# First sequence of a Fourier and feed-forward kernel: E as a spare row of Q, even products and table loads in another order

## The chip, the cores and the metric

The kernel runs on one core of one Trainium2 chip. The core has five engines that each work through their own queue in order: TensorE (PE, matrix products), VectorE (DVE), ScalarE (ACT), GpSimd (POOL) and SyncE (SP, which here only issues transfers). The metric is the time on the device in microseconds (us), the median over several executions. A profile is one execution recorded by the hardware profiler.

## The reference

What is computed, with eight sequences of 3008 rows and 256 columns:

```python
X = np.fft.fft(x, axis=1)
X = np.fft.fft(X, axis=2)
x = X.real.astype(np.float32).reshape(24064, 256)
h = x @ w_in            # 256 x 2048
r = np.maximum(h, 0.0)
g = r * r
out = (g @ w_out).astype(np.float32)   # 2048 x 256
```

## The kernel before, in words

**The mathematics.** Of the two Fourier transforms only the real part is wanted. The one along the columns is put into the weights: `G1` and `G2` (128 x 2048) are `w_in` multiplied by a cosine table `cosd` and a sine table `sind`. The one along the rows is done for each sequence as three arrays with 1505 columns, half of the frequencies: `Pt` (128 rows, cosine), `Qt` (127 rows, sine) and `Et`. E is the transform of one column of x alone (column 128, `H`), and it is needed on all 128 rows, because it enters the hidden layer as E times a number per row, `gE`. The hidden layer of a block of 251 columns and of 128 of the 2048 units is then `G1 . Pt` plus and minus `G2 . Qt` plus `gE * Et`; plus and minus give two output rows each.

**The transform of a sequence.** The rows of x are loaded four at a time (`load_x`, L145), as seven tiles: four tiles of even rows in three classes (`class_tiles`, L49) and three tiles, 4 to 6, of odd rows. `fold` (L352) adds and subtracts them on DVE into tiles `w`; a fold has a half for P (`for_p`: `f_s`, `f_sc`, `f_w`) and one for Q (`for_q`: `f_d`, `f_dc`, `f_w`). `dft_ops` (L447) makes from `w` and the tables `cosT` and `sinT` the groups of the transform. One group is for one of P, E, Q (`which` 0, 2, 1) and for even or odd frequencies (`kp`). It has five steps: `even_n` (L470), products of the even rows into one PSUM tile of the pool `psd`, tag "d", which has two buffers, and a copy `da` on ACT; `join_4` and `join_2` (L486 to L494), sums and differences on DVE; `odd_n` (L496), products of the odd rows into a PSUM tile of tag "h"; and `join_1` (L532), which writes the result. For E in the first sequence the same column of `w` is broadcast to 128 (L466), so that the product has E on all its rows. For the other seven sequences E is computed once for all, written to a DRAM tile `e_dram` (L548) and loaded with a broadcast (`load_e`, L551).

**Weights.** The weights come as 64-bit numbers and are rounded to 32 bits by `convert` (L230): two operations on DVE (L241, L246), three on ACT (L243, L244, L248), three on DVE (L251, L253, L254). `begin_win(j)` (L260) starts that for one of eight pieces of `w_in`, and issues its load unless it is loaded already, as pieces 0 to 2 are; `rounded(j)` ends it; then come products with `cosd` and `sind` (L269), copies `G` (L270), and two products with one column of the unit matrix for `gE` (L278). Pieces of `w_out` are loaded and converted by `load_wout` (L286).

**The order of the first sequence.** From L730 on the order is written out by hand; each engine keeps it. `awake(n)` (L193) puts n products of the unit matrix, whose result nobody uses, into PE's queue. `groups_at` calls steps by number: 0 to 9 are P, 10 to 19 E, 20 to 29 Q, five for each kp. The core of it:

```python
    load_table(cosT, cos_s, (0,))        # behind load_x(0, 4)
    ...
    groups_at(0, 5)                      # P, even products
    awake(12)
    ...
    groups_at(10, 15, 4)                 # E, even products; P, last join
    ...
    groups_at(9, 13, 18, 11, 12, 16, 17, 14)
```

**Steps.** A step works on one block of 251 columns and two times 128 hidden units (`j`, eight of them). `front` (L555) makes two pairs of products `ph` (L565, L566) and on DVE `he` (L568) and two `g` (L570, L571); the first `he` needs the first 251 columns of `Pt`, `Qt` and `Et`, and `gE`. `combine` (L578) has relu and square on ACT (L580, L581). `back` (L596) multiplies by `w_out`, two steps later; from the second block on with seven products instead of eight, whose sums of `g` are made on POOL (L588 to L591). In the first eight steps `weights` (L802) also converts the remaining pieces: in step 0 it ends piece 2 of `w_in` and begins piece 3, in step 1 it begins the first piece of `w_out` and piece 4, and so on. In all later steps the folds and groups of the next sequence are spread between the steps.

**Transfers.** Nearly all are issued by SP, one after the other; `cosd`, `sind` and its last column by ACT. A transfer signals on one of eight semaphores in turn, and the issue waits until the one before it on the same semaphore has landed. For the first sequence SP issues x tiles 0, 1, the first weights, x tiles 2 to 4, then the tables of cosine between x tiles 5 and 6, the rest of cosine, sine, and weights as their buffers come free.

Of the kernel before, what the change touches and what calls it, by code (L numbers as in the profile page):

```python
# [12 lines left out]
PSUM = bass.MemoryType.PSUM  # L13
P = 128
R = 32

# [63 lines left out]
def kernel(  # L82
# [100 lines left out]
                                     in_=src[mine[0]:mine[0] + step * (m - 1) + 1:step, :, i, 0:nk])  # L183

    make_identity(nc, ident)
    ramp = const.tile([P, 2], F32, name="ramp")
    nc.vector.memset(ramp[:, 0:1], 1151.0)
    nc.vector.memset(ramp[:, 1:2], 255.0 * 2.0 ** 23)
# [71 lines left out]
    def begin_win(j):  # L260

        w = ep.tile([P, 2, CH], F32, name="win", tag="sB" if j % 2 else "sA")
        finish = convert(parts(w, 1), win.pop(j, None) or load(pair_in(j)))

        def products():
            for tab, G, nm in ((cosd, G1, "mC"), (sind, G2, "mD")):
                pg = psm.tile([P, CH], F32, name="pg", tag=nm)
                for i in range(2):
                    nc.tensor.matmul(pg, tab[:, i], w[:, i], start=i == 0, stop=i == 1)  # L269
                nc.scalar.copy(G.rearrange("p (h j f) -> j p h f", h=2, j=NJ)[j],  # L270
                               pg.rearrange("p (h f) -> p h f", h=2))

        def for_e():

            ps = psd.tile([P, CH], F32, name="pe", tag="d")
            for h in range(2):
                fc = j + NJ * h
                nc.tensor.matmul(ps[:, h:h + 1], G2[:, fc * P:(fc + 1) * P], ident[:, P - 1:], start=True, stop=True)  # L278

            return lambda: nc.vector.tensor_scalar_mul(gE[:, j::NJ], ps[:, 0:2], 0.5)  # L280

        win[j] = finish, products, for_e
# [48 lines left out]
    NE = B - 1  # L331
    xe = const.tile([P, 4, NT, NE], F32, name="xe")
    we = const.tile([P, 2, NT, NE], F32, name="we")
    e_dram = dp.tile([NE, NKT], F32, name="e_dram")
    nc.gpsimd.memset(xe, 0.0)

    def load_column(t):
# [14 lines left out]
    def fold(b, t):  # L352
# [42 lines left out]
        def f_w(part=slice(0, D)):  # L395
            v, w = st["sc"], w_of(t)
            for kp in range(2):
                tt(out=w[r, kp, part], in0=v[r, 0, part], in1=v[r, 1, part], op=ALU.subtract if kp else ALU.add)

        if b == 0:  # L400
            return [f_s, f_d, f_sc, f_dc, lambda: f_w(PART[0]), lambda: f_w(PART[1])]
        ops = [(0.9, f_s), (0.9, f_d), (0.7, f_sc), (0.6, f_dc), (1.1, f_w)]
        if not odd or t == ODD0:
            return ops, None
# [42 lines left out]
    def dft_ops(b):  # L447
# [2 lines left out]

        def start():
            PQE[b] = [pq.tile([n, NKT], F32, name=nm, tag=nm)
                      for nm, n in (("Pt", P), ("Qt", P - 1), ("Et", P))]

        def group(kp, which):
            n = NE if b is None else P - 1 if which == 1 else P
            tab = sinT if which == 1 else cosT
            n2, _, n1, n0 = NC[kp]
            st = {}

            def product(ps, c):
                ts = [t for t in range(NT) if TILES[t][0] == c]
                for t in ts:
                    rows = TILES[t][3]
                    w = we[0:rows, kp, t] if b is None else folded[b, t][0:rows, kp, PART[which % 2]]
                    w = w[:, H:H + 1].to_broadcast([rows, n]) if which == 2 and b is not None else w[:, 0:n]  # L466
                    nc.tensor.matmul(ps, w, tab[0:rows, kp, PLACE[t]:PLACE[t] + NC[kp][c]],  # L467
                                     start=t == ts[0], stop=t == ts[-1])

            def even_n():  # L470
                st["ps"] = psd.tile([P, 512], F32, name="pd", tag="d")[0:n]
                a = st["a"] = hp.tile([P, 2 * P], F32, name="da", tag="da", bufs=2)[0:n]
                for c, at, nk in ((0, 0, n2), (1, n2, n2), (2, 2 * n2, n1)):
                    product(st["ps"][:, at:at + nk], c)
                nc.scalar.copy(a[:, 0:n2], st["ps"][:, 0:n2])

            def both(lo, hi, a, ps):

                nk, nh = a.shape[-1], hi.shape[-1]
                tt(out=lo, in0=a, in1=ps, op=ALU.add)  # L480
                if which == 1:
                    tt(out=hi[:, ::-1], in0=ps[:, 0:nh], in1=a[:, 0:nh], op=ALU.subtract)
                else:
                    tt(out=hi[:, ::-1], in0=a[:, 0:nh], in1=ps[:, 0:nh], op=ALU.subtract)
# [8 lines left out]
                st["c"] = hp.tile([P, NC[0][3]], F32, name="dc2", tag="dc2", bufs=2)[0:n, 0:n0]  # L493
                both(st["c"][:, 0:n1], st["c"][:, n1:n0], a, ps[:, 2 * n2:2 * n2 + n1])  # L494

            def odd_n():  # L496

                pool, tag = (psh, "h") if b == 0 else (psd, "d")
                ps = pool.tile([P, 512], F32, name="pd", tag=tag)[0:n]
                st["odd"] = ps[:, 0:n0]  # L500
                if not b:
                    return product(ps[:, 0:n0], 3)
                nq = (n0 + 2) // 2 if kp else (n0 + 1) // 2
                for part in range(2):
                    if kp:
                        tab, o = (cosT, sinT)[part], 0
                        to = ps[:, part * nq:part * nq + nq]
                        other = part != which
                    else:
                        tab, o = (cosT, sinT)[which], part  # L510
                        to = ps[:, part:n0:2]
                        other = part != which
                    for i, pair in enumerate(((ODD0, ODD0 + 1), (ODD0 + 2, NT))):
                        nc.tensor.matmul(to, folded[b, pair[other]][:, kp, PART[which]][:, 0:n],  # L514
                                         columns(tab, ODD0 + i, o), start=i == 0, stop=i == 1)
                if kp:
                    st["cos"] = hp.tile([P, nq], F32, name="oc", tag="oc", bufs=1)[0:n]
                    nc.scalar.copy(st["cos"], ps[:, 0:nq])
                    st["sin"] = ps[:, nq:2 * nq]
# [9 lines left out]
                else:  # L529
                    tt(out=o[:, 1::2], in0=a[:, 1:nq], in1=ps[:, 1:nq], op=ALU.subtract)  # L530

            def join_1():  # L532
                dst = PQE[1][2][0:n] if b is None else PQE[b][which]
                nh = S // 8
                both(dst[:, kp:kp + 2 * n0 - 1:2], dst[:, M - kp - 2 * (nh - 1):M - kp + 1:2], st["c"],
                     st["odd"])

            ops = [(0.1, even_n), (0.4, join_4), (0.5, join_2), (0.1, odd_n), (0.8, join_1)]
            if b and kp:
                ops.insert(4, (0.5, join_odd))  # L540
            return ops

        ops = [] if b is None else [(0.0, start)]
        for which in (2,) if b is None else (0, 1) if b else (0, 2, 1):
            for kp in range(2):
                ops += group(kp, which)
        if b is None:
            ops.append((0.0, lambda: nc.sync.dma_start(out=e_dram[:, :], in_=PQE[1][2][0:NE])))  # L548
        return ops

    def load_e(b):  # L551
        nc.sync.dma_start(out=PQE[b][2], in_=e_dram[b - 1:b].to_broadcast([P, NKT]))


    def front(b, k0, n, j, between):  # L555
# [4 lines left out]
        for h in range(2):  # L560
            fc = j + NJ * h
            fs = slice(fc * P, (fc + 1) * P)
            ps = psh.tile([P, 2, CH], F32, name="ph", tag="h")
            hP, hQ = ps[:, 0, 0:n], ps[:, 1, 0:n]
            nc.tensor.matmul(hP, G1[:, fs], pt[:, ks], start=True, stop=True)  # L565
            nc.tensor.matmul(hQ, G2[0:P - 1, fs], qt[:, ks], start=True, stop=True)  # L566
            t = hp.tile([P, CK], F32, name="he", tag="he")[:, 0:n]
            nc.vector.scalar_tensor_tensor(out=t, in0=et[:, ks], scalar=gE[:, fc:fc + 1], in1=hP,  # L568
                                           op0=ALU.mult, op1=ALU.add)
            tt(out=g[:, h, 0, 0:n], in0=t, in1=hQ, op=ALU.add)  # L570
            tt(out=g[:, h, 1, 0:n][:, ::-1], in0=t, in1=hQ, op=ALU.subtract)  # L571
            between()
# [162 lines left out]
    for_p(1)  # L735
    begin_win(0)
    load_x(0, 2)
    for dst, src in ((cosd, cos_d), (sind[:, :, 0:P - 1], sin_d), (sind[:, :, P - 1:], alt_d)):
        nc.scalar.dma_start(out=dst, in_=src.rearrange("(c p) m -> p c m", p=P))
    load_x(0, 3)  # L740
    load_x(0, 4)
    load_table(cosT, cos_s, (0,))
    load_x(0, 5)
    load_table(cosT, cos_s, (1,))
    load_x(0, 6)
    load_table(cosT, cos_s, range(2, NT))
    load_table(sinT, sin_s, range(ODD0, NT))
    win[1] = load(pair_in(1))
    load_table(sinT, sin_s, range(ODD0))
# [3 lines left out]
    win[0][1]()  # L753
    awake(10)
    for_p(3)
    groups_at(0, 5)
    awake(12)
    for_q(1)
    for_p(4)
    for_p(5)  # L760
# [3 lines left out]
    for_q(4)  # L764
    groups_at(6, 7)
    for_q(5)
    groups_at(10, 15, 4)
    for_q(6)
    groups_at(9, 13, 18, 11, 12, 16, 17, 14)
    awake(4)  # L770
    groups_at(23)
    begin_win(1)
    groups_at(19, 28)
    copy_e = win[0][2]()
    for_q(3)
    groups_at(20, 25)
    awake(10)
    begin_win(2)
    rounded(1)
    groups_at(21, 22, 24, 26, 27, 29)  # L780
    copy_e()
    LAG = 2
    BLOCKS = [(k0, min(CK, NKT - k0)) for k0 in range(0, NKT, CK)]
    steps = [(b, k0, n, j) for b in range(B) for k0, n in BLOCKS for j in range(NJ)]
# [136 lines left out]
```

## Time and profile before

| | us |
|---|---|
| median of 6 executions | 1953.1 (1951.96 to 1954.88) |
| the profiled execution | 1952.9 |
| its span, from the first to the last instruction | 1951.1 |
| PE busy | 1936.4 (99%) |
| DVE busy | 1398.7 (72%) |
| ACT busy | 924.1 (47%) |
| POOL busy | 1173.1 (60%) |
| first `he` of the first step | 53.16 |

How to read the lines of the profile. A line of a timeline has the start, the duration, the engine, the line of the kernel, the operation and tiles (out <- in, partitions x elements), how many records it merges, and in brackets how long the engine had been idle just before, and what ended that wait. A product in 32-bit floating point shows as two records. A line of the waits has who waited for whom: us in total, times, the longest. A row of the table by stage has for each engine its busy time in the stage and the number of records, then the clock that TensorE was granted (PEclk, 1.00 is full), the share of the 16 transfer engines that were busy, and GB/s.

### The profile page before, as it was taken

The page shows a single profiled execution, that of the slowest core. Times are in us where ns is not written, and L with a number is a line of the kernel's source. Part 1 is how long each engine was busy: PE and PEld are TensorE (multiplying, and loading weights), DVE is VectorE, ACT ScalarE, POOL GpSimd, SP SyncE. Part 2 cuts the span into 40 slices and gives each one's busy share as a digit, 9 for nine tenths or more (in the row PEclk, how much of TensorE's full clock was granted, in tenths as well). Part 3 has the DMA queues.
Part 4 walks back from the last instruction along what each step waited for, and adds up shares of the span by engine and source line. Part 5 has one row for each costly group of instructions (what it writes and reads, how often), then busy time and mean ns, then how long its engine had stood idle before and what let it go on. Part 6 is the DMA issues. An engine that isn't in the chain of part 4 may idle for free.

```text
span 1951.1 us, 27794 instructions
## 1 busy us (share of the span) xinstructions
PE 1936.4 (99%) x9296; PEld 1722.7 (88%) x9296; DVE 1398.7 (72%) x3442; ACT 924.1 (47%) x1068; POOL 1173.1 (60%) x1705
## 2 busy tenths in 40 slices
PE   8999999999999999999999999999999999999998
PEld 7888888888988889888998889888898888988887
DVE  7998966777677776777767776677767777655654
ACT  1754544445444544445444444444544454445443
POOL 0037746676567665676557665666756676566655
PEclk9999999999999999999999999999999999999999
DMA  7332102111011111111011200121002101100101
GB/s 209 98 45 52 33 9 55 33 27 28 14 46 33 38 20 27 41 35 33 12 35 37 45 19 11 37 53 28 20 13 55 33 11 22 24 15 12 21 12 22
DMA packets 145387, 68.90 MB, mean 35 GB/s; under 512 B 129049, under 2 KB 136156, under 8 KB 145243
## 3 DMA queue, kind: packets, MB, share of 16 engines
q1 hardware_dynamic: 144144, 66.60, 15.3%
q8 instruction: 73, 1.20, 0.3%
q10 hardware_dynamic: 1099, 0.52, 0.1%
q14 instruction: 71, 0.58, 0.1%
HBM read 42.39 MB, written 24.68 MB: 34 GB/s over the span
## 4 chain that ended last, share of the span: by engine, by line
PE 96%; DVE 2%; DMA 1%; issue 0%; SPq 0%; ACT 0%; DVEq 0%
PE ph L566 16%; PE ph L565 16%; PE mC L618 16%; PE mA L618 16%; PE mB L618 16%; PE mD L618 8%; PE pd L467 3%; PE pd L514 2%; PE filled L195 1%; DMA cosT<-in_cos_s_dram 0%; DVE m L253 0%; DVE fd L251 0%; DVE he L568 0%; PE mA L605 0%; PE mB L605 0%
## 5 line engine op out<-in xcount | busy, mean ns | idle before, releaser
L580 ACT ACTIVATE g<-g 128x1004 f32<-128x1004 f32 (+1 forms) x384 | 399.4, 1040 | 792.0 <-DVE g L571 426.1
L588 POOL TENSOR_TENSOR s<-g 128x251 f32<-128x251 f32 (+1 forms) x376 | 247.2, 657 | 710.7 <-ACT g L581 649.2
L568 DVE SCALAR_TENSOR_TENSOR he<-Et,gE,ph 128x251 f32<-128x251 f32 (+1 forms) x768 | 362.0, 471 | 413.5 <-PE ph L566 411.0
L565 PE MATMUL ph<-Pt,G 128*128 128x251 f32 (+1 forms) x1536 | 451.3, 375 | 0.0
L566 PE MATMUL ph<-Qt,G 127*128 127x251 f32 (+1 forms) x1536 | 451.2, 374 | 0.0
L581 ACT ACTIVATE g<-g 128x1004 f32<-128x1004 f32 (+1 forms) x384 | 399.3, 1040 | 12.2
L618 PE MATMUL mC<-s,wsum 128*128 128x251 f32 (+1 forms) x1504 | 381.4, 374 | 0.0
L618 PE MATMUL mA<-g,wout 128*128 128x251 f32 (+1 forms) x1504 | 379.9, 374 | 0.0
L570 DVE TENSOR_TENSOR g<-he,ph 128x251 f32<-128x251 f32 (+1 forms) x768 | 320.5, 417 | 55.7 <-POOL s L588 1.4
L566 PEld LDWEIGHTS ph<-Qt,G 127*128 127x128 f32 x1536 | 291.3, 190 | 35.8
L565 PEld LDWEIGHTS ph<-Pt,G 128*128 128x128 f32 x1536 | 287.4, 189 | 35.2 <-DVE g L571 0.9
L618 PEld LDWEIGHTS mC<-s,wsum 128*128 128x128 f32 x1504 | 285.6, 190 | 34.6
L618 PEld LDWEIGHTS mA<-g,wout 128*128 128x128 f32 x1504 | 282.9, 189 | 35.8 <-issue 1.3
L571 DVE TENSOR_TENSOR g<-he,ph 128x251 f32<-128x251 f32 (+1 forms) x768 | 314.2, 409 | 0.0
L590 POOL TENSOR_TENSOR s<-g 128x251 f32<-128x251 f32 (+1 forms) x376 | 306.1, 814 | 0.0
L589 POOL TENSOR_TENSOR s<-s,g 128x251 f32<-128x251 f32 (+1 forms) x376 | 275.3, 732 | 29.5
L591 POOL TENSOR_TENSOR s<-g,s 128x251 f32<-128x251 f32 (+1 forms) x376 | 254.1, 676 | 0.0
L618 PE MATMUL mB<-g,wsum 128*128 128x251 f32 (+1 forms) x752 | 220.5, 374 | 0.0
L618 PE MATMUL mD<-s,wout 128*128 128x251 f32 (+1 forms) x752 | 220.4, 374 | 0.0
L618 PE MATMUL mB<-s,wout 128*128 128x251 f32 (+1 forms) x752 | 219.9, 374 | 0.0
L618 PEld LDWEIGHTS mB<-g,wsum 128*128 128x128 f32 x752 | 142.6, 190 | 17.4
L618 PEld LDWEIGHTS mD<-s,wout 128*128 128x128 f32 x752 | 141.9, 189 | 17.7
(120 smaller groups left out, 1315.5 us busy)
## 6 DMA issues: line engine op xcount, KB each, us to landing
out_dram<-os SPq DMA_DIRECT2D x376, 56.0 KB
xt<-in_x_dram SPq DMA_DIRECT2D x32, 384.0 KB
xt<-in_x_dram SPq DMA_DIRECT2D x42, 128.0 KB
Et<-e_dram SPq DMA_DIRECT2D x7, 752.5 KB
xt<-in_x_dram SPq DMA_DIRECT2D x9, 512.0 KB
out_dram<-os SPq DMA_DIRECT2D x288, 6.8 KB
raw<-in_moe_w_in_dram SPq DMA_DIRECT2D x16, 256.0 KB
raw<-in_moe_w_out_dram SPq DMA_DIRECT2D x16, 256.0 KB
```

The source lines that it names most:

```text
L565: nc.tensor.matmul(hP, G1[:, fs], pt[:, ks], start=True, stop=True)
L566: nc.tensor.matmul(hQ, G2[0:P - 1, fs], qt[:, ks], start=True, stop=True)
L568: nc.vector.scalar_tensor_tensor(out=t, in0=et[:, ks], scalar=gE[:, fc:fc + 1], in1=hP, op0=ALU.mult, op1=ALU.add)
L570: tt(out=g[:, h, 0, 0:n], in0=t, in1=hQ, op=ALU.add)
L571: tt(out=g[:, h, 1, 0:n][:, ::-1], in0=t, in1=hQ, op=ALU.subtract)
L580: act(v, v, AF.Relu)
L581: act(v, v, AF.Square)
L588: gt(out=s1, in0=g21, in1=g22, op=ALU.add)
L589: gt(out=s2, in0=s1, in1=g11, op=ALU.subtract)
L590: gt(out=s3, in0=g11, in1=g21, op=ALU.subtract)
L591: gt(out=s4, in0=g12, in1=s2, op=ALU.subtract)
L618: nc.tensor.matmul(acc[nm][:, i, 0:n], w, v[:, 0:n], start=j == 0 and i == 0, stop=j == NJ - 1, skip_group_check=True)
```

## The change

- **E as Q's free row.** Q's products have 127 rows; now `Qt` has 128, and the last is E. The weights for it are tiles `lone` with 128 columns, all zero but the last, which lie in `wsum` (not yet used then); the last column is the middle column of `w`, with a sign for each class, copied by ACT (`f_e`). For Q's two kp the products of `lone` with `cosT` start the sums in PSUM, and Q's own products with `sinT` are added to them. As E has to be joined with other signs than Q, the joins multiply by a number per row, `signs`, in one instruction.
- **Spreading E.** The first 251 columns are spread to all rows of `Et` by one product with the last column of the unit matrix (`spread_e`) and a copy on ACT. The other 1254 columns go by two transfers on SP, one row out to `e_dram` and a broadcast back (`spread_rest`). These are issued where the prologue ends, ahead of the loads that the steps issue.
- **Order.** Q's eight steps for each kp are now `even_n, join_4, join_2, odd_n, join_lo, even_e, odd_e, join_hi`, numbers 10 to 17 and 18 to 25. E's even products (15, 23) come right behind P's even products, in place of twelve unused products; `gE` of piece 0 comes ahead of the even products of Q. The unused products go from 48 + 10 + 12 + 4 + 10 to 48 + 10 + 14.
- **Tables.** All even rows of the cosine table are issued ahead of x tiles 5 and 6, the first two pieces ahead of x tile 4 too.

The diff, cut to its core:

```diff
+    signs = const.tile([P, 2], F32, name="signs")
+    for i in range(2):
+        nc.vector.tensor_scalar(out=signs[:, i:i + 1], in0=last, scalar1=(-2.0, 2.0)[i], scalar2=(1.0, -1.0)[i],
+                                op0=ALU.mult, op1=ALU.add)
+    lone = wsum.rearrange("p a j h -> p (a j) h")
+    nc.gpsimd.memset(lone[:, 0:2 * NT], 0.0)
...
-            ps = psd.tile([P, CH], F32, name="pe", tag="d")
+            ps = psd.tile([P, CH], F32, name="pe", tag="d") if j else psm.tile([P, CH], F32, name="pe", tag="mC")
...
+        def f_e():
+            nc.scalar.mul(lone[r, 2 * t:2 * t + 2, P - 1:], w_of(t)[r, :, H:H + 1], -1.0 if TILES[t][0] else 1.0)
...
+            def even_e():
+                st["ps"] = psd.tile([P, 512], F32, name="pd", tag="d")
+                for c, at, nk in EVEN:
+                    product(st["ps"][:, at:at + nk], c, True)
...
+                if both_in:
+                    join = nc.vector.scalar_tensor_tensor
+                    if only != 1:
+                        join(out=lo, in0=ps, scalar=signs[:, 0:1], in1=a, op0=ALU.mult, op1=ALU.add)
+                    if only != 0:
+                        join(out=hi[:, ::-1], in0=a[:, 0:nh], scalar=signs[:, 1:2], in1=ps[:, 0:nh],
+                             op0=ALU.mult, op1=ALU.add)
+                    return
...
+                pool, tag = (psd, "d") if b != 0 else (psm, "mA") if kp == 0 and both_in else (psh, "h")
...
+    def spread_e():
+        _, qt, et = PQE[0]
+        ps = psd.tile([P, CH], F32, name="pe", tag="d")[:, 0:CK]
+        nc.tensor.matmul(ps, last.to_broadcast([P, P]), qt[:, 0:CK], start=True, stop=True)
+        nc.scalar.copy(et[:, 0:CK], ps)
+    def spread_rest():
+        _, qt, et = PQE[0]
+        nc.sync.dma_start(out=e_dram[0:1], in_=qt[P - 1:P])
+        nc.sync.dma_start(out=et[:, CK:], in_=e_dram[0:1, CK:].to_broadcast([P, NKT - CK]))
...
     load_x(0, 2)
+    load_x(0, 3)
     for dst, src in ((cosd, cos_d), (sind[:, :, 0:P - 1], sin_d), (sind[:, :, P - 1:], alt_d)):
         nc.scalar.dma_start(out=dst, in_=src.rearrange("(c p) m -> p c m", p=P))
-    load_x(0, 3)
+    load_table(cosT, cos_s, (0, 1))
     load_x(0, 4)
-    load_table(cosT, cos_s, (0,))
+    load_table(cosT, cos_s, (2, 3))
     load_x(0, 5)
-    load_table(cosT, cos_s, (1,))
     load_x(0, 6)
-    load_table(cosT, cos_s, range(2, NT))
+    load_table(cosT, cos_s, range(ODD0, NT))
...
-    groups_at(0, 5)
-    awake(12)
+    groups_at(0, 5, 15, 23)
...
-    groups_at(10, 15, 4)
+    groups_at(4, 16, 24)
     for_q(6)
-    groups_at(9, 13, 18, 11, 12, 16, 17, 14)
-    awake(4)
-    groups_at(23)
+    groups_at(13, 21, 9)
+    copy_e = win[0][2]()
     begin_win(1)
-    groups_at(19, 28)
-    copy_e = win[0][2]()
     for_q(3)
-    groups_at(20, 25)
-    awake(10)
+    groups_at(10, 18)
+    awake(14)
+    rounded(1)
     begin_win(2)
-    rounded(1)
-    groups_at(21, 22, 24, 26, 27, 29)
+    groups_at(11, 12, 14, 19, 20, 22)
+    spread_e()
+    groups_at(17, 25)
     copy_e()
+    spread_rest()
```

## The prediction, made before the changed kernel had run

> **What bounds the kernel now.** I read the page first, then the waits of TensorE (PE), then the timelines of PE, VectorE (DVE), ScalarE (ACT) and SyncE's queue (SP) over the first 110 us. All times in us, from the span's start.
>
> ```profile
> PE 1936.4 (99%) x9296; PEld 1722.7 (88%) x9296; DVE 1398.7 (72%) x3442; ACT 924.1 (47%) x1068; POOL 1173.1 (60%) x1705
> ```
>
> PE is busy 99% of the span. Where does it still wait? The waits of PE:
>
> ```profile
> PE pe L278 <- ACT G L270: 2.7, 2, 2.2
> PE pg L269 <- DMA cosd<-in_cos_d_dram: 2.6, 1, 2.6
> PE pd L467 <- DVE dc L482: 1.5, 1, 1.5
> PE mA L605 <- DVE wout L254: 1.5, 4, 0.6
> ```
>
> All of these lie before 104 us. The timeline of PE:
>
> ```profile
> 17.47 2.04 PE L269 MATMUL pg<-win,cosd 128*128 128x256 f32 x4 [2.65 <-DMA cosd<-in_cos_d_dram]
> ...
> 29.37 9.95 PE L467 MATMUL pd<-cosT,w 128*128 128x377 f32 x40
> ...
> 62.51 0.60 PE L278 MATMUL pe<-ident,G 128*128 128x1 f32 x4 [2.21 <-ACT G L270]
> ...
> 103.58 0.69 PE L605 MATMUL mA<-g,wout 128*128 128x251 f32 x2 [0.56 <-DVE wout L254]
> ```
>
> After 103.58 PE shows no idle time until the last 5 us. So whatever the first sequence gains or loses by then reaches the end one for one, and nothing else of the change matters. Up to there DVE sets the pace, as its timeline shows:
>
> ```profile
> 26.07 0.25 DVE L480 TENSOR_TENSOR db<-da,pd 128x95 f32<-128x95 f32 x1 [2.79 <-ACT da L475]
> ...
> 53.16 0.48 DVE L568 SCALAR_TENSOR_TENSOR he<-Et,gE,ph 128x251 f32<-128x251 f32 x1 [1.59 <-PE ph L566]
> ...
> 57.42 0.42 DVE L241 TENSOR_SCALAR fd<-raw 128x512 uint32<-128x512 uint32 x1
> ```
>
> From 53.16 (the first `he`, my mark) to the last weights at 103.53 DVE has no visible gap. So I work out when the first `he` starts in the changed kernel, and what is lost between it and 103.53. Third, the clock, in the table by stage (the last three figures of a row: PEclk, DMA share, GB/s):
>
> ```profile
> 46.00:48.00 2.00, 0.93 (x6) 0.96 (x7) 1.90 (x6) 0.00 (x0) 0.00 (x0) 0.89 0.00 0
> 48.00:50.00 2.00, 2.00 (x10) 2.00 (x9) 0.57 (x3) 0.86 (x2) 0.00 (x0) 0.50 0.00 0
> 50.00:52.00 2.00, 2.00 (x16) 2.00 (x16) 1.53 (x5) 1.30 (x2) 0.00 (x0) 0.76 0.00 0
> ```
>
> An idle time of only 1.53 (45.54 to 47.07) brought 3.4 us at half clock; the longer one before 17.47 brought 6.8 us at half clock (0.50 to 0.71 from 16.8 to 23.6).
>
> **Removed.** E's twelve joins leave DVE: four `db` at 0.25, four `dc` at 0.35 and four `Et` at 0.54 come at their pitch to 0.97 + 0.97 + 0.92 + 0.92 = 3.8, with two waits (0.53 and 0.22) between them. Twelve filler products go net (84 to 72), and two copies of E's sums (0.24) leave ACT. E's 28 products stay on PE with the same columns: 2 x 1.09 even, 2 x 1.91 odd (from the 9.95 row, 40 records for six such pieces).
>
> **Added, at nothing.** ACT gets seven copies of two columns. No row has one; ACT's 0.24 for 95 columns bounds each, and ACT stands idle 4.17 and 7.38 before its `da` copies. Without that cover they would cost 7 x 0.24 = 1.7. GpSimd (POOL) gets one memset of 1792 columns; from its 0.20 (128) and 0.26 (196) I estimate 1.7, while it has nothing to do until 110. Twelve joins of Q turn from TENSOR_TENSOR into SCALAR_TENSOR_TENSOR: 471 against 417 ns at 251 columns, so +0.055 each, 0.5 ahead of the first `he`; it is in the sum.
>
> **Moved: the transfers.** `cosd` is issued by ACT at 12.56. It waits there for a cosine piece which is itself behind 512 KB of x and lands at 12.54 (by the landings that the trace records); then it shares the engines with the last x tile and lands at 17.34, `sind` with its last column at 18.3. In the changed order six small cosine pieces go ahead of x tile 4, so that wait should be over when ACT ends its `raw` at 11.98, and x tiles 5 and 6 come later. Bounds for `cosd`: 12.0 + 4.8 (same delay) = 16.8, and 12.0 + 3.0 (the 256 KB of weights issued at 62.67 landed at 65.69, alone) = 15.0. I take 15.3, nearer the second, and 16.4 for `sind`, since x tile 5 can only be issued at about 13.2. The x tiles then land about 17.5 and 19; DVE wants them at 18.43 and 21.61.
>
> **The new order, step by step.** PE: `pg` from 15.3, ten fills (0.22 each) to 19.5, P's even sums to 21.7, against 26.6 now. DVE ends its folds at 23.2 and finds `da` ready: the idle 2.79 is gone. Its joins free P's two even sums at 24.2 and, one fold (1.59) later, at 26.75. **Here is the new wait**: E's even products use the same pool of two buffers (tag "d"), so the two pieces can't start before 24.3 and 26.9. P's odd products stand behind them in PE's queue, and DVE's join of P behind those. PE idles about 4 of 5.2 us there, more than twice what already brought half clock at 47.5. At half clock E's second piece ends at 29.1 (28.0 at full), P's odd sums at 31.7 and 33.6. From there PE runs without a stop: 4 x 1.91 for E and Q odd, 0.36, 2 x 1.12 for Q even = 10.2, to 43.8. ACT's copy makes 44.3; DVE joins Q's second half (0.56 + 0.71 + 0.60, behind the first half's) to 46.9; fourteen fills end at 47.0; the product that spreads E takes 0.43, the first `front` pair 0.86, 0.2 to DVE: **first `he` at 48.5**. With the edges of the 3.4 us clock periods placed otherwise I get up to 49.9; I take 49.0, a gain of 4.2 against 53.16. At full clock throughout it would be 46.3.
>
> [...]
>
> **The price on SP's queue.** Now SP issues win[3], the first wout, win[4] and the second wout between 33.9 and 38.6, long ahead of need. In the changed program the write of E's row and the load that spreads it stand ahead of all of these, and the write waits for Q's last join, which ends 0.6 before the first `he` (call that end T). The steady state has both: the e_dram write landed 2.03 after its issue, the Et load of 752 KB 3.8 after its own. So: write landed T+2.1; load issued, win[3] issued T+2.55; the load (5/6 of the size) moves until about T+5.3; win[3]'s two halves, 0.7 each behind it, have landed by T+7.1. DVE wants win[3] 4.26 after the first `he` (57.42 - 53.16), at T+4.86. **Stall 2.2.** Bounds: 1.4 if the two transfers don't hinder each other (the pair at 62.67 had landed 3.7 after the first issue: T+6.3), 2.7 if they do more. What follows is 0.7 per half later and is wanted 3.3, 6.0 and 11 later: no stall.
>
> ACT's conversion of win[3] and the copies of G wait behind it, so PE's idle 2.21 before 62.51 becomes about 4.4, surely enough for half clock: 1.7 to 3.4 of PE's time, against PE's own slack further on of 0.15 + 0.39 + 0.40 + 0.56 = 1.5. That leaves 0 to 1.9; I take 0.2, since DVE and not PE paces those steps.
>
> **Sum**: -4.2 + 2.2 + 0.2 = -1.8. The profiled execution took 1952.9 (span 1951.1 and 1.8 around it), 0.2 under the median of 1953.1: **1951.1**.
>
> **Rivals.** (1) *The clock stays full in the buffer gap*: first `he` 46.3, -6.9 + 2.2 = -4.6, 1948.3. [...] Against: the 1.53 row. 15%. (2) *The table's early rows buy nothing*: `cosd` lands at 16.8 or later, PE passes to half clock at 16.8 as now, first `he` 50 to 51; -2.7 + 2.2 + 0.2: 1952.6. For it: the transfer engines are at a share of 0.85 or more from 2 to 28. 20%. (3) *Slower, by PE's clock in the steps*: if half clock after the stall lasts 6.8 us (as after 16.8), PE loses 3.4 and is late itself at 103.58; with a first `he` at 49.9 and the 2.7 stall: -3.3 + 2.7 + 1.9 = +1.3, 1954.2. It decides from the point where PE's lag passes its slack of 1.5. 11%. A small rest, 2%, has the stall several times longer than any row here.
>
> **Chances.** The forecast, 1950.2 to 1952.2, 52%. Range 1948.2 to 1954.3, which takes in the three rivals. About 0.2% (3.9 us) is what a measurement of this kernel can tell from no change. Faster than 1949.2: most of rival 1 and a tail of the forecast, 0.18; slower than 1957.0: 0.03; between, 0.79.
>
> **What would show it.** Right: DVE's first `he` near 49; in PE's timeline an idle time before E's first and second even piece, put down to DVE's `dc`, and PEclk 0.5 from about 24 to 30; SP's e_dram write just after Q's last join and the win[3] issues behind it; DVE idle about 2 before the `fd` of win[3], put down to a DMA. Wrong: win[3] issued before the write; no idle time on DVE there; PEclk at 1.00 all the way; the mark above 51, or any new idle time of PE after 104.

## The result, and the profile after

After: 1954.13 us (median of 36 executions, 1951.08 to 1956.61); before, measured beside it: 1951.84 (72 executions, 1948.13 to 1956.43). Ratio 1.0011, 95% interval 1.0007 to 1.0016: the change costs 2.2, where 1.8 of gain was forecast. The profiled execution took 1953.32 (span 1951.5), 0.42 more than that of before.

The page's busy times of after:

```profile
PE 1934.8 (99%) x9274; PEld 1720.3 (88%) x9274; DVE 1396.2 (72%) x3432; ACT 925.2 (47%) x1074; POOL 1174.2 (60%) x1706
```

DVE lost 2.5 of work and PE 1.6, and still the kernel is later. The waits of PE in after:

```profile
PE pe L289 <- ACT G L281: 4.9, 2, 4.5
PE pg L280 <- DMA sind<-in_alt_d_dram: 2.4, 1, 2.4
...
PE pd L488 <- DVE dc L524: 1.2, 1, 1.2
PE pg L280 <- DMA cosd<-in_cos_d_dram: 0.9, 1, 0.9
```

The wait for `cosd` fell from 2.6 to 0.9, but the last column of `sind` has one of its own, and the wait for `G` grew from 2.7 to 4.9. The timeline of PE in after:

```profile
15.19 1.10 PE L280 MATMUL pg<-win,cosd 128*128 128x256 f32 x4 [0.87 <-DMA cosd<-in_cos_d_dram]
18.64 1.54 PE L280 MATMUL pg<-win,sind 128*128 128x256 f32 x4 [2.35 <-DMA sind<-in_alt_d_dram]
...
26.22 1.33 PE L488 MATMUL pd<-cosT,wsum 95*128 95x95 f32 x8 [0.43 <-ACT wsum L412]
28.78 1.87 PE L488 MATMUL pd<-cosT,wsum 95*128 95x94 f32 x8 [1.23 <-DVE dc L524]
...
62.15 1.01 PE L289 MATMUL pe<-ident,G 128*128 128x1 f32 x4 [4.47 <-ACT G L281]
...
103.26 0.69 PE L674 MATMUL mA<-g,wout 128*128 128x251 f32 x2
```

That of DVE in after, of which only the lines with idle time that matter are shown:

```profile
19.41 0.69 DVE L379 TENSOR_TENSOR fs<-xt 128x512 f32<-128x512 f32 x1 [1.02 <-DMA xt<-in_x_dram]
...
25.02 0.25 DVE L520 TENSOR_TENSOR db<-da,pd 128x95 f32<-128x95 f32 x1 [0.74 <-ACT da L506]
...
33.73 0.55 DVE L520 TENSOR_TENSOR Pt<-dc,pd 128x377 f32<-128x377 f32 x1 [3.51 <-PE pd L488]
...
45.04 0.32 DVE L515 SCALAR_TENSOR_TENSOR db<-pd,signs,da 128x95 f32<-128x95 f32 x1 [2.96 <-ACT da L506]
...
50.59 0.48 DVE L637 SCALAR_TENSOR_TENSOR he<-Et,gE,ph 128x251 f32<-128x251 f32 x1 [0.65 <-PE ph L635]
...
57.08 0.43 DVE L252 TENSOR_SCALAR fd<-raw 128x512 uint32<-128x512 uint32 x1 [2.14 <-DMA raw<-in_moe_w_in_dram]
```

The first `he` is 2.57 earlier than in before's profile (50.59 against 53.16). Behind it stands the new stall for the weights, 2.14. Two other idle times have grown: 3.51 ahead of `Pt` (0.20 in before), for PE, and 2.96 ahead of Q's first `db` (1.32 in before), for ACT's copy of PE's sums. They come to 6.5, 5.0 more than in before, while the twelve joins of E that left DVE were worth 3.8. The queue of SP in after shows what the weights waited behind:

```profile
49.90 0.25 SPq L617 DMA_DIRECT2D e_dram<-Qt  x1
51.23 0.36 SPq L618 DMA_DIRECT2D Et<-e_dram  x1
51.64 1.20 SPq L237 DMA_DIRECT2D raw<-in_moe_w_in_dram  x2
```

And the table by stage of after (PEclk is the third figure from the end):

```profile
19.00:21.00 2.00, 2.00 (x9) 1.80 (x8) 1.52 (x4) 0.47 (x2) 0.00 (x0) 0.54 1.03 229
21.00:23.00 2.00, 2.00 (x13) 2.00 (x12) 1.93 (x6) 0.00 (x0) 0.00 (x0) 0.61 1.09 296
...
29.00:31.00 2.00, 2.00 (x9) 1.78 (x9) 1.15 (x4) 0.00 (x0) 0.00 (x0) 0.60 0.80 174
...
62.00:64.00 2.00, 1.85 (x6) 1.69 (x7) 1.93 (x5) 1.97 (x5) 0.00 (x0) 0.50 0.10 27
```

Three pauses, three stretches at half clock: 19.2 to 22.6, 29.4 to 32.8, 60.1 to 66.9.

### The profile page after: what moved, and what is told of

Its sections match the earlier page's. It is cut to its first block, busy times and chain, and to the rows that moved or that the text cites. A ratio compares the mean times of both kernels' runs of the same rounds, so it can differ in the third digit from the quotient of the medians.

```text
span 1951.5 us, 27742 instructions
## 1 busy us (share of the span) xinstructions
PE 1934.8 (99%) x9274; PEld 1720.3 (88%) x9274; DVE 1396.2 (72%) x3432; ACT 925.2 (47%) x1074; POOL 1174.2 (60%) x1706
## 4 chain that ended last, share of the span: by engine, by line
PE 97%; DVE 1%; DMA 1%; ACT 0%; SPq 0%; issue 0%; DVEq 0%
PE ph L634 17%; PE ph L635 17%; PE mC L687 16%; PE mA L687 16%; PE mB L687 16%; PE mD L687 8%; PE pd L488 3%; PE pd L563 2%; PE mA L674 1%; PE mB L674 1%; PE pg L280 1%; DMA xt<-in_x_dram 1%; DMA sind<-in_alt_d_dram 0%; DMA raw<-in_moe_w_in_dram 0%; PE filled L206 0%; DVE w L409 0%
## 5 line engine op out<-in xcount | busy, mean ns | idle before, releaser
L658 POOL TENSOR_TENSOR s<-s,g 128x251 f32<-128x251 f32 (+1 forms) x376 | 275.2, 732 | 29.4
```

Source lines behind the costliest of these rows:

```text
L658: gt(out=s2, in0=s1, in1=g11, op=ALU.subtract)
```

## The experiments

How they are read: in five series of runs 147 executions of before were taken beside the experiments, each with its mean granted clock. Sorted by it, 66 are at 0.999 or 1.000, mean 1949.38, and 64 at 0.997 or less, mean 1953.86; 17 at 0.998 lie between, 1951.0. The most frequent values are 0.999 (59 executions) and 0.995 (30). Time at half clock gives these figures: the profile of before has 6.8 + 3.4 and 2.3 at its end, 12.5 in 1951; half of that is lost, 0.32%, and its mean is 0.997. So the table has, beside the ratio to all of before, the mean over that of before's executions at 0.999 or more **in the same series**, which also takes out the difference between chips. Its 95% interval is 0.5 (e9 to e12) to 1.5 (e2) to either side. Below, "before at full clock" means these executions; 0.999 is not quite full, as the seven at 1.000 take 1948.2 on average.

| run | median, us | ratio to before, 95% | over before at full clock | first `he` of its profile |
|---|---|---|---|---|
| e1 | 1951.52 | 1.0004 (0.9995 to 1.0013) | +2.1 | 51.10 |
| e2 | 1953.95 | 1.0018 (1.0009 to 1.0026) | +4.1 | 52.69 |
| e3 | 1951.99 | 1.0002 (0.9992 to 1.0012) | +2.3 | 47.74 |
| e4 | 1954.21 | 1.0020 (1.0010 to 1.0030) | +4.8 | 49.52 |
| e5 | 1952.12 | 1.0002 (0.9993 to 1.0011) | +1.9 | 50.33 |
| e6 | 1949.73 | 0.9989 (0.9981 to 0.9998) | -0.1 | 49.56 |
| e7 | 1953.41 | 1.0009 (1.0000 to 1.0018) | +3.7 | 49.37 |
| e9 | 1949.68 | 0.9990 (0.9981 to 0.9999) | +0.9 | 50.04 |
| e10 | 1949.57 | 0.9991 (0.9980 to 1.0002) | +0.8 | 49.39 |
| e11 | 1948.76 | 0.9983 (0.9974 to 0.9992) | -0.1 | 48.27 |
| e12 | 1949.08 | 0.9988 (0.9979 to 0.9997) | +0.3 | 49.16 |
| e13 | 1945.99 | 0.9970 (0.9961 to 0.9980) | -2.9 | 48.33 |
| e14 | 1946.55 | 0.9978 (0.9970 to 0.9987) | -2.9 | 46.20 |
| e15 | 1949.03 | 0.9991 (0.9983 to 1.0000) | -0.1 | 49.24 |
| e16 | 1949.34 | 0.9987 (0.9978 to 0.9996) | +0.1 | 49.26 |
| e17 | 1947.17 | 0.9973 (0.9964 to 0.9981) | -2.2 | 46.85 |
| e18 | 1945.71 | 0.9968 (0.9956 to 0.9980) | -3.6 | 45.72 |

**One part undone or one gap filled (e1 to e4), from the changed kernel.** e1 issues the load of `win[3]`, the fourth piece of `w_in`, ahead of the two transfers of E's row:

```diff
     copy_e()
+    win[3] = load(pair_in(3))
     spread_rest()
```

> The changed kernel, with win[3]'s load issued ahead of the two transfers that spread E; nothing else differs. Queue theory (the stall of 2.14 us before the fd of win[3] is the price): the stall goes, PE's idle 4.47 us in step 1 shrinks to about 2.3, the first he stays at 50 to 51, and the time falls by 2 to 3.5 us against the changed kernel, to between 1.5 us under and 0.5 us over the kernel before. Theory of the early order (the x tiles and the last column of sind come later, E's even products wait for a buffer): the stall is hidden by something else, the time stays within 1 us of the changed kernel, about 2 us over the kernel before.

e2 puts the loads of x and of the tables back into before's order.

> The changed kernel with the transfers of the first sequence in their old order (x tiles 3 and 4 behind the issues of cosd and sind, cosine's even rows spread between x tiles 4 to 6 again). Theory of the early order, loads: DVE's wait of 1.02 us for x tile 5 goes, cosd lands near 17.3 again, the first he comes 0 to 1 us earlier than in the changed kernel's profile (50.59), the time falls by up to 1 us. Queue theory: the stall stays at 2.1, the time stays within 0.7 us of the changed kernel. If the new load order is worth something after all, the time rises by 1 us or more.

e3 takes E's even sums away from behind P's:

```diff
-    groups_at(0, 5, 15, 23)
+    groups_at(0, 5)
+    awake(12)
...
-    groups_at(4, 16, 24)
+    groups_at(4, 15, 23, 16, 24)
```

> The changed kernel with E's even products put behind P's odd products, just ahead of E's odd ones, and twelve unused products back in their old place. Theory of the early order, buffers: DVE's idle 3.51 us before Pt shrinks to below 2 and the first he comes about 1 us earlier (49 to 50.2, by the phase of the clock); the time falls by 1 us. Queue theory: the stall of 2.1 stays as it is, whatever the first he gains is kept, so the time still lies 0.5 to 1.5 us over the kernel before. If the early place is worth what it is there for, the time rises.

e4 fills PE's gap in step 1 with `awake(18)`.

> The changed kernel with eighteen unused products in PE's queue in step 1, where PE idles for 4.47 us and passes to half clock; the stall itself is not touched. Clock theory (it is the half clock after the stall that costs, because PE is then late itself): PEclk stays at 1.00 from 58 to 70 us and the time falls by 1 to 2 us. Queue theory: DVE sets the pace of these steps, PE catches up unseen, and the time stays within 0.5 us of the changed kernel.

The stall is real: without it 2.7 less (e1 against e4, which stands where after does; 95% interval 1.3 to 4.1). The half clock behind it costs nothing as long as the stall covers it: in e4 it is gone (PEclk 1.00 from 56 to 64) and the time is what after has (1954.21 and 1954.13). Without the stall it does cost: in e1's profile half clock from 60.5 to 67.3 (a pair of products of 251 columns takes 1.04 there, 0.59 before and behind it) makes PE late itself. From the first `he` (51.10) to the product that stands at 103.58 in before, e1 takes 51.31, and before 50.42:

```profile
102.41 0.59 PE L674 MATMUL mA<-g,wout 128*128 128x251 f32 x2
```

The old loads make no difference that is resolved (e2, 0.7 less than e4 by the means, within 1.8). e3 gains 2.2 on e4 (2.5 by the means, within 1.7), with the stall of 2.46 still in it; from its profile, DVE:

```profile
47.74 0.47 DVE L637 SCALAR_TENSOR_TENSOR he<-Et,gE,ph 128x251 f32<-128x251 f32 x1 [0.65 <-PE ph L635]
...
54.54 0.43 DVE L252 TENSOR_SCALAR fd<-raw 128x512 uint32<-128x512 uint32 x1 [2.46 <-DMA raw<-in_moe_w_in_dram]
```

**Both gains together, and the clock held (e5 to e8).** e5 is e1 and e3 in one.

> The changed kernel with both of the edits that helped: win[3]'s load ahead of the transfers that spread E, and E's even products behind P's odd ones with twelve unused products back. If the queue's stall (2.1 us) and the early even products (about 2 us) are two separate losses, they add up: 1949.5, about 1 us under the kernel before and 4 to 5 us under the changed kernel. If one of them hides behind the other, the time stays at 1951 to 1952, as with either alone.

They did not add up: 1952.12, where 2.7 and 2.2 off 1954.2 would make 1949.3. In its profile PE waits 3.59 for the last column of `sind`, and half clock from 20.1 on (the ten unused products at 20.78 take 3.71, in e11 2.40) puts the first `he` at 50.33. The clock, which comes and goes, is a part of what hid the sizes: e10 below, e5 with its gaps filled, stands at +0.8 where e5 has +1.9. The other part is not explained. e6 is before with its gaps filled by unused products: `awake(60)` for 48 at the start, `awake(6)` ahead of Q's second even group, `awake(8)` in step 1.

> The kernel before, with unused products in the three places where PE idles in its profile: twelve ahead of the products with cosd, six between Q's two even pieces, eight in step 1. Nothing else is touched. Clock theory (the profile that I predicted from had two stretches of half clock that most executions do not have, so its first he at 53.2 is a late one): the mean granted clock is 0.999 in nearly all executions, the spread shrinks from 8 us to about 3, the first he comes at 49 to 50, and the median falls by 1 to 2 us, to that of the better half of the executions before, 1949 to 1949.5. Rival (the spread has nothing to do with PE's idle times): the spread and the median stay.

e7 is the changed kernel with its gaps filled: 52 for 48, ten between the products with `cosd` and `sind`, 14 and 5 ahead of E's even sums, 18 in step 1.

> The changed kernel with unused products in its idle places of PE: four more ahead of cosd, ten between the products with cosd and sind, fourteen and five ahead of E's two even pieces, eighteen in step 1. The stall of win[3] is not touched. Clock theory: the mean granted clock rises to 0.998 to 0.999, the first he comes at 47.5 to 48.5, and the time falls by 2 us or more against the changed kernel, to 1951 to 1952, but stays 1 to 2 us over the filled kernel before, because the stall of 2.1 us takes more than the first he gains (48.7 to 47.6 by the durations at full clock). If the half clock costs nothing here, the time stays at 1954.

e8 is before, unchanged, profiled once more.

> The kernel before, unchanged, for another profile of it. By the mean clocks that each execution lists, 17 of 31 were at 0.999 or 1.000 and 1948 to 1950.5. With that chance this profile has no half clock from 16.8 to 23.6 us nor from 47.5 to 51, DVE's wait of 2.79 us before its first join is short or gone, and the first he starts at 49 to 50.5 rather than 53.16.

e8 settled what the profile of before had been. It took 1948.32. Its timeline of PE:

```profile
17.46 1.10 PE L269 MATMUL pg<-win,cosd 128*128 128x256 f32 x4 [2.83 <-DVE fs L368]
...
44.16 1.32 PE L467 MATMUL pd<-sinT,w 95*127 95x94 f32 x8 [1.52 <-DVE dc L482]
```

The same two pauses, 2.83 (its end is put down to DVE here, and the products with `cosd` start at 17.46, in the first profile at 17.47) and 1.52, where the first profile had 2.65 and 1.53. But its table by stage:

```profile
18.00:20.00 2.00, 2.00 (x13) 1.65 (x12) 1.93 (x7) 0.74 (x2) 0.00 (x0) 1.00 0.74 198
...
46.00:48.00 2.00, 2.00 (x19) 1.96 (x18) 1.90 (x7) 1.68 (x3) 0.00 (x0) 1.00 0.00 0
```

against the first profile of before:

```profile
18.00:20.00 2.00, 2.00 (x6) 1.61 (x5) 1.91 (x6) 0.37 (x1) 0.00 (x0) 0.50 0.85 242
```

and DVE in e8:

```profile
48.61 0.47 DVE L568 SCALAR_TENSOR_TENSOR he<-Et,gE,ph 128x251 f32<-128x251 f32 x1 [0.64 <-PE ph L566]
```

The first `he` is at 48.61 instead of 53.16, 4.55 earlier, and the whole execution is 4.58 shorter. e6 agrees: with the gaps filled none of its executions is under 0.998, and it stands level with before at full clock. Its first `he` is at 49.56, and that of e16, the same kernel, at 49.26: e8 is one of the fastest executions of before. e7 gained less than expected: with the clock full all through the first sequence the changed kernel still stands at +3.7, against +4.8 in e4.

**The parts at full clock (e9 to e12).** e9 is e7 with `win[3]` loaded right ahead of the two transfers, as in e1, and 8 instead of 18 in step 1.

> The changed kernel with unused products in PE's gaps (52 instead of 48 first, ten between the products with cosd and sind, 14 and 5 ahead of E's even sums, 8 in step 1) and with the load of the fourth piece of w_in issued behind the two transfers of E's row instead of ahead... that is, issued by hand directly ahead of none of them: the call stands right behind them is not what is tried; it stands right ahead of them. Beside e7 (1953.41, first he 49.37) only the stall goes. Theory (the clock lost in before's profile made its first he late; the queue's stall is a real cost of about 2.3 at any clock): first he 49.4 as in e7, no idle time of DVE before the fd of win[3], 1951.1. Rival (the stall is hidden at full clock, what costs is the joins and buffers of Q's row): within 0.5 of e7, 1953.

e10 also has E's even sums where e3 has them, behind 18 unused products.

> As e9, and E's two even sums stand directly ahead of the even sums of Q again (behind P's last join) instead of right behind P's; 18 unused products stand in their old place. New order of the loads kept. Theory (the buffers that E's sums wait for hold up P's odd sums and DVE's joins by about 2): first he 47.3 to 48.3, 1949.3 to 1950.2, level with before filled (1949.7). Rival (what is left of the loss is the late x tile 5, which DVE waits for): first he 49 or later and 1951.

e11 is the row alone: e10 with before's loads, `awake(60)` first, none between `cosd` and `sind`, and 12 behind P's even sums.

> E as Q's free row alone, at full clock: as e10, but with the order of the loads of x and of the cosine table of before, 60 unused products first, none between cosd and sind, 12 behind P's even sums. Beside before filled (1949.73, first he 49.56; 48.61 in the look at before with full clock) this has twelve joins of E fewer on DVE and Q's joins 0.055 longer each. Theory (the row is worth what it saves on DVE ahead of the first he, between 1 and 1.5, once stall, buffer wait and clock are out of the way): first he about 47.2, 1948.2 to 1948.8. Rival (DVE's work saved is off the path, PE's 28 products and the x tiles set the pace): first he 48.6 or later, 1949.7 or more.

e12 is the loads alone: e6 with the changed order of x and tables, 52 first and ten between `cosd` and `sind`.

> The new order of the loads alone: before with its gaps filled (e6, 1949.73, first he 49.56), the x tiles and cosine tables issued as in the changed kernel, 52 unused products first and ten between cosd and sind. Theory (cosd comes 2 earlier, but x tile 5 lands about 2 later and DVE, which sets the pace, waits 1 to 2 for it): first he 49.0 to 50.5, 1949.5 to 1951. Rival (cosd earlier by 2 moves the whole prologue, as forecast): first he below 48, 1948.2 or less.

The stall at full clock costs 2.8 (e7 to e9, 3.7 to 0.9; DVE's idle time in e7 is 2.37). e10 stands where e9 does, and its first `he` came at 49.39, not at 47.3 to 48.3: with the gaps filled, the late place of E's even sums gains nothing, though it had in e3. (18 unused products take the place of the sums there, and DVE waits 1.11 for x tile 5.) The loads alone are worth nothing (e12 +0.3): `cosd`'s products start at 15.90, and DVE, which sets the pace, gains nothing by it. e11's 1948.76 lies in the range that the theory gave, but on that chip before at full clock had 1948.87: the row alone gains nothing there, and its rival was nearer. That e11 is 0.9 under e10 is no price of the loads, as e11 also has six unused products fewer behind P's even sums. (e7 and e9 are no clean price of the whole change at full clock: their products ahead of E's even sums lie in PE's queue themselves; P's odd sums start 8.6 behind its even ones in e7, 7.0 in after.)

**Where the row's gain is (e13 to e18).** DVE has 5.14 of idle time in e11 ahead of Q's first `db`:

```profile
42.72 0.32 DVE L515 SCALAR_TENSOR_TENSOR db<-pd,signs,da 128x95 f32<-128x95 f32 x1 [5.14 <-ACT da L506]
```

So I suspected PE's queue. e13 makes only the first product of each class of E (`for t in ts[:1] if lone_e else ts`); E lacks a part of its sum.

> As e11 (E as Q's free row alone, gaps filled; first he 48.27, DVE idle 5.14 ahead of Q's first db), but of E's fourteen products only the first of each class is made: six are left out, so E lacks a part of its sum and the output is not the reference's. They take about 2.9 of PE's time by their rows (two even at 0.29, four odd at 0.64), nothing else changes. Theory (from P's joins on PE's products in their order set the pace, and the DVE time that the row saves turns into idle time ahead of Q's first db): first he about 45.4, that idle time down to about 2.2, the time 2.9 less than e11 again in the same call. Rival (DVE's folds and joins or the weights set the pace, PE only looks busy): first he within 0.5 of 48.3, the time unchanged.

e14 is e11 without `awake(12)` behind P's even sums.

> As e11 without the twelve unused products behind P's even sums, which take 2.67 of PE's queue (24.45 to 27.12 in e11). Theory (PE's queue sets the pace from there): everything behind moves up by 2 to 2.6, as P's odd sums have their rows at 23.2: first he 45.7 to 46.3, clock still full since no idle time of PE over 1 appears, the time 2 to 2.6 under e11 again and under the fast half of before by as much. Rival (the place of the unused products only turns into a wait for DVE's folds, as the queue needs their results): PE idle 2 or more near 25, half clock near 27, first he 48 or later, the time within 0.5 of e11 again or above it.

e15 is e11 again, e16 is e6 again.

> e11 once more, beside before filled on the same chip, since e6 and e11 ran on different ones. Theory (the row alone is worth nothing: against the executions of before with a clock of 0.999 or more in its own call e11 stood at -0.1 and e6 at -0.1): within 0.5 of e16. Rival (the row alone is worth 1, as 1948.76 against 1949.73 reads): 0.8 to 1.5 under e16.

> e6 once more, as the measure for the three above on the same chip. Both: within 0.5 of the executions of before at a clock of 0.999 or more, none of its executions under 0.998.

e17 is e16 without the same `awake(12)`, the control of e14.

> The control of e14: before filled (e16) without the same twelve unused products. Theory (in before DVE sets the pace from P's joins to Q's; it can gain no more than its idle times there, 0.20 + 0.53 + 0.22 + 1.32 = 2.3, and PE then waits for it): first he 47.0 to 48.8 against 49.26, 0.5 to 2.2 under e16, and less than the 2.8 that e14 gained on e15. Rival (the twelve products are on the path in any case, and the row has no part in it): 2.6 or more under e16, level with e14 at 3 under the executions of before at 0.999 or more.

e18 is e14 with `awake(3)` for the `awake(10)` behind piece 0's products.

> e14 with 3 instead of 10 unused products behind the products with cosd and sind of piece 0. Theory (PE still sets the pace; DVE's idle time of 1.29 ahead of its first db is what can go before the last fold, which ends at 23.1, is the limit): first he 44.8 to 45.5 against 46.20, 0.7 to 1.4 under e14. Rival (P's odd sums then wait for tile 6 of x and PE has a gap that brings half clock): first he 46 or later, the time within 0.4 of e14 or above.

The row alone gains nothing here either: -0.1 (e15) against +0.1 (e16), in the same series. PE's queue is on the path: with 3.2 of its products less (E's take 2.81 instead of 5.99; 2.9 was expected) the time falls by 2.8 (e13 against e15, by the means, within 0.9). The profiled execution of e13 is one of two in twelve that took 1948.8 and more, with half clock from 20.1 and a late first `he`; its idle time ahead of Q's `db`, 1.97, is as expected. And the unused products, put there to hold the clock, lie on that path too. PE in e14, one block of products behind the other, where e11 had 2.84 of unused ones between P's even and odd sums:

```profile
20.64 2.39 PE L206 MATMUL filled<-ident 128*128 128x128 f32 x20
22.88 6.15 PE L488 MATMUL pd<-cosT,w 95*128 95x95 f32 x28
28.86 6.15 PE L488 MATMUL pd<-cosT,wsum 95*128 95x95 f32 x28
34.84 3.97 PE L488 MATMUL pd<-sinT,w 128*127 128x377 f32 x12
```

and DVE in e14:

```profile
40.65 0.32 DVE L515 SCALAR_TENSOR_TENSOR db<-pd,signs,da 128x95 f32<-128x95 f32 x1 [2.75 <-ACT da L506]
...
46.20 0.48 DVE L637 SCALAR_TENSOR_TENSOR he<-Et,gE,ph 128x251 f32<-128x251 f32 x1 [0.65 <-PE ph L635]
```

The control takes most of the credit away from the row: e17 gains 2.2 on e16 (from +0.1 to -2.2) by the same edit, the sum of DVE's idle times there, at the upper end of what was expected. DVE in e17 (in e16 the first of these idle times was 1.32):

```profile
41.19 0.25 DVE L480 TENSOR_TENSOR db<-da,pd 127x95 f32<-127x95 f32 x1 [0.21 <-ACT da L475]
...
46.85 0.47 DVE L568 SCALAR_TENSOR_TENSOR he<-Et,gE,ph 128x251 f32<-128x251 f32 x1 [0.64 <-PE ph L566]
```

With DVE almost without a pause up to there (0.47, 0.21 and 0.73), before should have little more to gain; the row still has 2.75 of idle DVE. So the row is worth some 0.7 (e14 -2.9, e17 -2.2, in two series and each within 0.7 to 1.0: not resolved). e18 stands 0.6 under e14, at the lower edge of what was expected and not resolved either; it is 1.4 under e17 (0.8 to 1.9, same series), but before with three unused products at that place was not run, so that is no price of the row. e18, with the row but neither the new loads nor the queue's stall, is faster than both kernels: 1945.71, 0.9968 of before (0.9956 to 0.9980).

## Why the prediction was wrong

The time lies 3.0 above the forecast and on the other side of before. It lies inside the range only by luck: the upper end of the range came from the third rival, whose mechanism did not happen.

**The step that failed is the -4.2**, "49.0, a gain of 4.2 against 53.16". Both of its figures failed. The 49.0 was 1.6 too early: the first `he` came at 50.59. The 53.16 came from one execution that had passed two stretches at half clock, which the prediction had itself read from the table by stage; it was taken for the kernel's own pace. In e8, at full clock up to there, before starts the first `he` at 48.61, and with its gaps filled at 49.56 and 49.26 (e6, e16), so even the forecast 49.0 was hardly a gain over before at full clock.

What each figure did to the result: of the 3.0, 1.6 is the first `he`, 0.8 is that the profiled execution of after (1953.32) was shorter than its median, and the rest are small terms behind the first `he`. Against the 1953.1 from which the prediction started, the change would so cost 1.0. The other 1.3 comes from the base: the median of the 72 executions of before beside after is 1951.84. The six that the prediction had were all at 1951.96 or more, their median agreed with the profile's 1952.9, and nothing in these times showed that 66 of 147 executions lie 4.5 below the slow ones; the mean of the 72 (1951.97) holds both kinds. After lies between 0.995 and 0.998 in all its 37 executions. Against before at full clock the change costs 4.8 (1954.14 on average, less 1949.38 from the five series; e4, beside such executions, has the same 4.8), before itself loses 2.6 on average to the clock, and the rest is the 2.2 that was measured.

Point by point:

- *What happens by 103.58 reaches the end one for one*: right. Before against e8: 4.55 at the first `he`, 4.58 in all. DVE does have a gap in between, 0.53 at 101.50, which the prediction overlooked; after has the same 0.53 at 101.19, so it cancels. After is 0.33 ahead of before's profile at that point; an idle 0.45 of PE at 174.86, for a late `g`, was not foreseen and turns that into some 0.2 behind. Whether the change is its cause is not shown.
- *`cosd` lands at 15.3*: right, 15.05. *`sind` with its last column at 16.4*: 18.50. *x tile 5 at 17.5*: 19.38, and DVE waited 1.02 for it. The pause of 2.35 for a column of 256 numbers brought 3.4 us of half clock; P's even sums ended at 25.8, not 21.7. As the wait for the buffers behind them was 2.3 shorter than forecast, about half of these 4.1 reached the first `he`: 2.1 against the 48.5 that was worked out, 1.6 against the 49.0 that was taken.
- *The wait for the pool's two buffers*: right in kind and place, shorter (0.43 and 1.23, not about 4 in all), because P's sums themselves were late. The 0.43 ends with ACT's last copies for E (`wsum`, L412), which the working had put at nothing; the buffer came free at about the same time (DVE's `dc` ends at 26.07). Half clock followed, to 32.8 and not about 30.
- *Removed, 3.8 of DVE*: right as work, wrong as time. PE's products were next: DVE's time came back as idle time ahead of `Pt` and of Q's `db` (e13, e14). I named no price for that, although the working said itself that PE "runs without a stop" from there.
- *The price on SP's queue, 2.2*: right; 2.14 in the trace, 2.7 and 2.8 in the time (e1, e9). The write was issued 0.03 behind Q's last join, and `win[3]` had landed 7.1 behind it (49.87 to 56.98), as worked out, but partly by luck: the write landed 1.3 after its issue, not 2.1, and `win[3]` was issued 1.8 behind the join, not 2.55, while the transfers then took as much longer.
- *PE's half clock behind the stall, 0.2*: 4.47 of idle time against 4.4, and 6.8 of half clock; its cost in after was nothing, as the shift of -0.33 passes it unchanged and e4 shows. It was a near thing: at 103.26 PE has no idle time left where before has 0.56, so its slack of 1.5 was used up, and in e1, without the stall, PE was late.
- *Rivals.* (1) fell: the clock did not stay full in after. (2), the early table rows buy nothing: its condition did not come true, `cosd` was early, but its substance did (e2, e12), and its first `he` of 50 to 51 is what the profile has. (3) gave 1954.2, nearly the time measured, by a mechanism that did not happen: PE is not late at 103.26, and e4 takes the half clock away without a gain. That number was luck.

One row, the 1.53, decided for the prediction that half clock follows a pause, and the same pause takes both answers. In one execution of before the clock fell to half within a pause of 2.65, for 6.8, and 0.47 behind one of 1.53, for 3.4; in another, e8, pauses of 2.83 and 1.52 brought no half clock (PEclk 1.00 from 16 to 24 and from 44 to 50). Nor does the length divide them: 1.23, 0.43 of idle time shortly before it, was followed by half clock in after, 2.84 in e18 was not. The traces show one regularity: in before and in after all changes of the granted clock lie on a grid of 3.413 us (in before 16.82, 23.65, 47.54 and 50.96, which are 2, 9 and 10 periods from the first; in after 19.16, 22.58, 29.41, 32.82, 60.12 and 66.95, which are 1, 3, 4, 12 and 14). What decides whether a pause is followed by half clock no run here shows. With the pauses filled it is rare: e6's executions are all at 0.998 or more, where 64 of the 147 of before are at 0.997 or less.

What stays open: how the 4.8 divides, besides the stall's 2.7 to 2.8, between after's half clock ahead of the first `he` (two stretches of 3.4, at most 3.4 of PE's time) and PE's queue; and why e3 gained by the late place of E's even sums while e10 did not. e7 and e9, meant for that, carried too many products of their own.

## What to carry to other kernels

Before a profile is taken as the base of a sum, look at its granted clock and at the mean clock of several executions: a stretch at half clock that other executions do not have (here 6.8 and 3.4, with none up to the first `he` in e8) belongs to the one execution, and a gain counted from it is not there in the others. When work leaves the engine that sets the pace, follow the next engine's queue through the same stretch, the unused products that hold its clock included; they cost their time as soon as that engine is the bound (twelve of them 2.2 in before, 2.8 with the row). A transfer that waits for late data belongs behind the loads in an in-order queue that do not; that placing alone was worth 2.7 here (1.3 to 4.1).

## What the hardware showed that I had not expected

- The executions of before, one and the same program, lie 4.5 apart by their mean clock: 66 of 147 at 0.999 and more, 64 at 0.997 and less.
- A pause of 1.23 following one of 0.43 within the same 3 us was followed by half clock (after, 29.4), while single pauses of 2.83 and 1.52 were not (e8), nor was one of 2.84 in e18.
- The last column of `sind`, 1 KB, landed 5.3 after its issue (13.19 to 18.50), 3.0 behind the 127 columns that ACT issued 0.85 earlier; in before the same transfer took 4.8 (13.57 to 18.32) and landed 0.4 behind those columns. In e5 PE waited 3.59 for it, until 19.51. A small transfer beside the tiles of x had no fixed duration here.
